# A recurrence followed by a cosine-gated product: the second part in groups of 512 tokens, its down product by halves of the features

## The chip, the cores and the metric

The kernel runs on one core of a Trainium2 chip. The metric is the device time of one execution in microseconds (us). Everything is computed in fp32. The engines are called as in the profile: PE (TensorE, the matmuls; its weight loads are shown apart as PEld), DVE (VectorE), ACT (ScalarE), POOL (GpSimd) and SP (SyncE, which here only issues DMAs).

## What is computed

The first part is a recurrence over 768 steps, for 4 batches and 8 heads of 40 features; its output `y`, turned to 3072 tokens of 320 features, goes through a second part with 2048 hidden features:

```
for t in range(S):                                  # r, k, v, w, a, b: [4, 8, 768, 40]
    y[:, :, t] = einsum('bhd,bhde->bhe', r_t, state)
    Sa = einsum('bhde,bhe->bhd', state, a_t)
    state = state * w_t - einsum('bhd,bhe->bhde', Sa, b_t) + einsum('bhd,bhe->bhde', v_t, k_t)
x = y.transpose(0, 2, 1, 3).reshape(3072, 320)
h = x @ w_in                                        # w_in [320, 2048], w_out [2048, 320]
out = (h * cos(h)) @ w_out
```

## The kernel before, in words

The recurrence goes in 24 chunks of 32 steps. A chunk's 128 partitions are (batch, step), so a chunk is 128 tokens. Three functions do a chunk:

- `prep(c)` does what doesn't need the state: it turns the six operands on PE (tiles `turned`), makes the decays (`wp`, `rw`, `wx` on DVE and POOL), the gram matrices (`gram`, masked into `pc`, `abd`, `rvbd`), and the inverse of a triangular matrix by five levels of squaring. A level is 8 matmuls `power` on PE, a copy on ACT (line 267), mostly an addition on DVE (271) and four 32x32 block transposes on DVE (253), and the next level's matmuls need these transposes.
- `chain(c)` does what needs the state: `x0ps`, `snps`, the state's update `upd`, `sTps`, `mps`, the outputs `yps`, the new state's transpose `strn`, and the seam `xps` (line 382), which turns the chunk's 128 tokens to `xT`, with features in the partitions. The last `xps` of a chunk is used below as the mark of that chunk.
- `mlp(c, xT)` (lines 391 to 424) does the second part for the chunk's 128 tokens. The up product `ph` (399) takes a block of 128 hidden features at a time: three matmuls accumulate over the 320 input features, which are cut in 128, 128 and 64. Each has a 128-column weight tile of `w_in` and a moving operand of 128 tokens. Four blocks fill one PSUM bank of 512 columns, and on these 512 columns the cosine is made: DVE 406, POOL 407, DVE 409 and 410, ACT 411 and 412, DVE 414, which writes `gT`. The down product `po` (416) takes 16 matmuls, each with a 128x128 tile of `gT` as weights and 320 columns of `w_out` moving, all into one bank; ACT copies that to `ot` (421), and four DMAs on SP's queue write it out.

Each fp32 matmul of the program is two passes in the trace (a weight load and a matmul each), so that a `power` level is 16 passes and a chunk's `ph` 96.

The weights arrive as fp64 words. `rounded` (lines 141 to 164) turns each of 28 pieces to fp32: a DMA on ACT's queue into `words`, three operations on DVE, three on POOL, one more on DVE, and a product on POOL into `w_in_sb` or `w_out_sb`.

The loop over c calls `chain(c)`, the loads of chunk c + 2, `prep(c + 1)` and `mlp(c)`. A scheduler then places the instructions in each engine's queue, so that matmuls of `mlp(c)` stand between those of `prep(c + 1)` and of `chain(c + 1)`. Each engine works its queue in order. PSUM has three banks for `prep`, two for `chain`, two for `ph` and one for `po`.

Of the kernel before, what the change touches and what calls it, by code (L numbers as in the profile page):

```python
# [23 lines left out]
def kernel(  # L24
# [39 lines left out]
    # K tiles of the first product of the second part  # L64
# [13 lines left out]
    def kept(name, shape, n=1, fill=None):  # L78
        """Buffers that are used in turn, with a fill that the parts never written keep."""
        tiles = []  # L80
        for i in range(n):
            t = const.tile(shape, F32, tag=f"{name}{i}", name=f"{name}{i}")
            if fill is not None:
                nc.vector.memset(t, fill)
            tiles.append(t)
        return tiles
# [34 lines left out]
    # the strict upper triangle, and of that the blocks on the diagonal  # L121
# [18 lines left out]

    def rounded(dst, src):
# [8 lines left out]
        frac = sb2.tile([P, 512], F32, tag="gT", name="frac")[:n, :cols]  # L150
# [44 lines left out]
    def prep(c):  # L195
        """What of a chunk doesn't need the state."""
# [3 lines left out]
        # products of w over the steps of each batch, by a scan that begins anew at each block  # L200
# [10 lines left out]
        # operands with the decay in them, with steps in the free dimension and in the partitions  # L211
# [13 lines left out]
        # N's transpose, compact, beside what becomes the inverse's transpose: I - N^T  # L225
# [163 lines left out]
    FG = 4  # L389
# [76 lines left out]
```

## Time and profile before

| | |
|---|---|
| time, median of 3 runs | 2125.78 us (2123.2 to 2127.21) |
| span of the profiled execution, first to last instruction | 2120.7 us |
| PE busy | 2016.7 us, 95% |
| PE weight loads | 1713.6 us, 81% |
| DVE, ACT, POOL busy | 936.2, 338.0, 217.5 us |
| mean granted PE clock | 0.70 of full |
| DMA | 40.33 MB, 19 GB/s |

The profile gives no other time of its own execution than the span; the span is 5.1 us under the median of the runs.

How to read it: a row of groups has the line, engine, operation, tiles and shapes, then busy time and mean of one, then the engine's idle time before these instructions and who ended it. The mean of a pass includes its way through the array, which overlaps the next pass; the pace of a stream is its length in a row of the timeline divided by the count, or busy time divided by the count. A row of the timeline has start, length, engine, line, operation, tiles, shapes and count, and in brackets idle time before it. A row of windows has a stretch, then for each engine busy time and number of instructions, then the PE clock granted, as a share of full speed, and DMA.

### The profile page before, as it was taken

To read this page: it belongs to the slowest core of one execution; us is meant where nothing else is said; L and a number is where in the kernel's file an instruction comes from. 1 tells how busy PE (TensorE), PEld (TensorE's weight loads), DVE (VectorE), ACT (ScalarE), POOL (GpSimd) and SP (SyncE) were. 2 spreads that over 40 slices of the span, in tenths; PEclk is the share of its full clock that TensorE was granted. 3 is DMA by queue.
4 is the path that set the end of the run, shared out by engine and by line. 5 is a ranking of instruction groups with operands and counts; after the bars stand their busy time and mean duration, and the time that the engine had idled before them with its cause. 6 is when DMAs were issued, how large, how long until landed. Compare 5 with 4: busy or idle time off the path is not lost.

```text
span 2120.7 us, 35848 instructions
## 1 busy us (share of the span) xinstructions
PE 2016.7 (95%) x15592; PEld 1713.6 (81%) x15592; DVE 936.2 (44%) x1671; ACT 338.0 (16%) x744; POOL 217.5 (10%) x365
## 2 busy tenths in 40 slices
PE   4777999999999999999999999999999999999997
PEld 4766888888888888888888888888888888888885
DVE  8765344343443443444434434444344443444432
ACT  0102112021111111211211102112111021121111
POOL 4662000000000000000000000000000000000000
PEclk8658577586675775866857767677586676776777
DMA  3331010010100100101001000010010000100000
GB/s 83 84 95 26 10 20 12 14 21 4 20 13 14 20 10 14 18 9 20 13 13 20 10 14 13 13 20 13 14 20 9 15 13 13 20 7 1 4 3 4
DMA packets 165211, 40.33 MB, mean 19 GB/s; under 512 B 158656, under 2 KB 161728, under 8 KB 165056
## 3 DMA queue, kind: packets, MB, share of 16 engines
q1 hardware_dynamic: 161280, 27.57, 7.9%
q10 hardware_dynamic: 3776, 10.49, 1.6%
q8 instruction: 123, 2.02, 0.4%
q14 instruction: 32, 0.26, 0.0%
HBM read 34.08 MB, written 3.93 MB: 18 GB/s over the span
## 4 chain that ended last, share of the span: by engine, by line
PE 85%; DVE 10%; ACT 3%; POOL 1%; issue 1%; POOLq 0%; ACTq 0%
PE ph L399 26%; PE power L89 18%; PE po L416 10%; PE yps L89 8%; PE x0ps L89 6%; PE gram L89 5%; PE strn L89 4%; DVE rw L207 4%; PE turned L192 3%; PE snps L89 2%; ACT snbd L308 2%; PE mps L89 1%; DVE wp L205 1%; PE sTps L89 1%; PE xps L382 1%; DVE mbd L346 1%
## 5 line engine op out<-in xcount | busy, mean ns | idle before, releaser
L399 PE MATMUL ph<-xT,w_in_sb 128*128 128x128 f32 (+1 forms) x2304 | 581.7, 388 | 0.5 <-ACT xT L384 0.5
L399 PEld LDWEIGHTS ph<-xT,w_in_sb 128*128 128x128 f32 (+1 forms) x2304 | 436.4, 249 | 134.5 <-issue 83.6
L89 PE MATMUL power<-pc,pbd 128*128 128x64 f32 (+1 forms) x1920 | 392.7, 387 | 25.7 <-DVE pbd L253 25.6
L89 PEld LDWEIGHTS power<-pc,pbd 128*128 128x128 f32 x1920 | 383.1, 305 | 34.3 <-issue 27.0
L416 PE MATMUL po<-w_out_sb,gT 128*128 128x320 f32 x768 | 261.2, 489 | 22.0 <-DVE gT L414 22.0
L253 DVE STREAM_TRANSPOSE pbd<-pc 32x256 f32<-32x256 f32 x480 | 208.4, 434 | 155.3 <-ACT pc L267 146.3
L416 PEld LDWEIGHTS po<-w_out_sb,gT 128*128 128x128 f32 x768 | 158.9, 218 | 91.8 <-DVE gT L414 28.1
L407 POOL TENSOR_SCALAR turns<-turns 128x512 f32<-128x512 f32 x96 | 59.3, 618 | 1193.1 <-DVE turns L406 1193.0
L406 DVE TENSOR_SCALAR turns<-ph 128x512 f32<-128x512 f32 x96 | 66.4, 691 | 210.4 <-PE ph L399 210.4
L267 ACT COPY pc<-power 128x256 f32<-128x256 f32 x96 | 35.8, 372 | 735.2 <-PE power L89 723.8
L271 DVE TENSOR_TENSOR pc<-power,pc 128x256 f32<-128x256 f32 x72 | 30.5, 424 | 275.8 <-ACT pc L267 275.7
L89 PE MATMUL yps<-kn,rvbd 128*128 128x40 f32 x384 | 97.8, 347 | 4.9 <-DVE mbd L346 4.8
L411 ACT ACTIVATE red<-red 128x512 f32<-128x512 f32 x96 | 60.7, 633 | 261.0 <-DVE red L410 261.0
L89 PE MATMUL yps<-bn,mbd 128*128 128x40 f32 x384 | 98.7, 350 | 0.0
L89 PE MATMUL strn<-ident,st 64*64 64x40 f32 x1472 | 96.7, 305 | 0.0
L89 PEld LDWEIGHTS strn<-ident,st 64*64 64x64 f32 x1472 | 93.3, 215 | 2.0
L89 PE MATMUL x0ps<-nat_v,abd 128*128 128x40 f32 x384 | 92.3, 416 | 0.0
L409 DVE SCALAR_TENSOR_TENSOR red<-turns,ph 128x512 f32<-128x512 f32 x96 | 65.8, 685 | 58.2 <-POOL turns L407 58.2
L89 PEld LDWEIGHTS x0ps<-nat_v,abd 128*128 128x128 f32 x384 | 85.3, 327 | 7.5 <-issue 5.4
L89 PEld LDWEIGHTS yps<-kn,rvbd 128*128 128x128 f32 x384 | 78.9, 254 | 11.2 <-DVE mbd L346 9.1
L89 PEld LDWEIGHTS yps<-bn,mbd 128*128 128x128 f32 x384 | 82.0, 264 | 0.0
L207 DVE RECIPROCAL rw<-wp 128x512 f32<-128x512 f32 x24 | 80.4, 3351 | 0.7
(113 smaller groups left out, 2013.8 us busy)
## 6 DMA issues: line engine op xcount, KB each, us to landing
words<-in_moe_w_out_dram ACTq DMA_DIRECT2D x16, 320.0 KB, 3.0
words<-in_moe_w_in_dram ACTq DMA_DIRECT2D x8, 512.0 KB, 4.2
nat_w<-in_w_dram SPq DMA_DIRECT2D x96, 40.0 KB, 2.1
nat_k<-in_k_dram SPq DMA_DIRECT2D x96, 40.0 KB, 2.1
nat_a<-in_a_dram SPq DMA_DIRECT2D x96, 40.0 KB, 2.1
nat_b<-in_b_dram SPq DMA_DIRECT2D x96, 40.0 KB, 2.2
nat_v<-in_v_dram SPq DMA_DIRECT2D x96, 40.0 KB, 2.0
nat_r<-in_r_dram SPq DMA_DIRECT2D x96, 40.0 KB, 2.1
```

Of the source, the lines that this page charges most:

```text
L89: nc.tensor.matmul(o, lhsT=lhsT, rhs=rhs, start=start, stop=stop, skip_group_check=True)
L192: nc.tensor.transpose(ps[:, q, :], x[:, q, :], ident)
L207: nc.vector.reciprocal(seq(rw), wp)
L253: nc.vector.transpose(pbd[blk[i], :, :, blk[i]].rearrange("p e q t -> p (e q) t"), heads(pc)[blk[i], :, 0, :],)
L267: nc.scalar.copy(heads(new)[:, :, 0, :], ps[:, :, 0, :])
L308: nc.scalar.copy(snbd[blk[i], i], ps[blk[i]])
L399: nc.tensor.matmul(ph[:, f, :], lhsT=w_in_sb[: d1 - d0, i, cols], rhs=xT[: d1 - d0, i, :], start=i == 0, stop=i == len(KT) - 1,)
L406: nc.vector.tensor_scalar(n, h, 1.0 / (2.0 * math.pi), ROUND, ALU.mult, ALU.add)
L407: nc.gpsimd.tensor_scalar(n, n, -ROUND, 1.0, ALU.add, ALU.mult)
L409: nc.vector.scalar_tensor_tensor(red, n, -TWO_PI_HI, h, ALU.mult, ALU.add)
L411: nc.scalar.activation(red, red, ACTF.Abs)
L416: nc.tensor.matmul(po, lhsT=gT[:, f, :], rhs=w_out_sb[:, f0 + f, :], start=f0 + f == 0, stop=f0 + f == NF - 1,)
```

## The change

The second part waits until four chunks (512 tokens, one group) are through the seam, and then works for all of them:

- `xT` holds four chunks, `[128, 3, 4, 128]`; `chain` writes its quarter.
- `mlp_up` does one block of 128 hidden features for 512 tokens: three matmuls with a moving operand of 512 columns, in place of twelve with 128. The cosine on 512 columns is as before. A block's `gT` has a buffer of its own, eight in all (`gT0` to `gT7`), each single.
- `mlp_down` does eight blocks for one chunk. The first half of the features is copied from PSUM to `ot` by ACT; the second is added to `ot` by DVE, and the DMAs follow.
- `mlp_part(s)` spreads a group's work over four chunks: up for blocks 0 to 7, down for these (four chunks), up for 8 to 15, down for these. Group 0's parts are called behind chunks 4 to 7, and the last group's parts behind the last chunk.
- To make room, `words` shares the two buffers of `rvbd`, `frac` uses `gT0` and `gT1`, `snT` shares `vT`'s buffer, and the state's update is made in place, without `tmp`.

```diff
-        words = sb2.tile([P, 512, 2], I32, tag="words", name="words")[:n, :cols]
+        words = sb2.tile([P, 512, 2], I32, tag="rvbd", name="words")[:n, :cols]
...
-    def mlp(c, xT):
+    def mlp_up(j, f, xT):
+        ph = ps_h.tile([P, GC * P], F32, tag="h", name="ph")
+        for i, (d0, d1) in enumerate(KT):
+            nc.tensor.matmul(
+                ph, lhsT=w_in_sb[: d1 - d0, i, f * P : (f + 1) * P],
+                rhs=xT[: d1 - d0, i, :, :].rearrange("p c t -> p (c t)"),
+                start=i == 0, stop=i == len(KT) - 1,
+            )
...
+        nc.vector.tensor_tensor(gT_b[j], ph, red, ALU.mult)
+    def mlp_down(g, cc, fh):
+        c = g * GC + cc
+        po = ps_o.tile([P, DM], F32, tag="o", name="po")
+        for j, f in enumerate(range(fh * FH, (fh + 1) * FH)):
+            nc.tensor.matmul(
+                po, lhsT=gT_b[j][:, cc * P : (cc + 1) * P], rhs=w_out_sb[:, f, :],
+                start=j == 0, stop=j == FH - 1,
+            )
+        if fh == 0:
+            nc.scalar.copy(ot_b[cc], po)
+            return
+        nc.vector.tensor_tensor(ot_b[cc], po, ot_b[cc], ALU.add)
...
+    def mlp_part(s):
+        g, cc = s // GC - 1, s % GC
+        if not 0 <= g < NG:
+            return
+        fh = cc // 2
+        if cc % 2 == 0:
+            for j, f in enumerate(range(fh * FH, (fh + 1) * FH)):
+                gT_b[j] = sb1.tile([P, GC * P], F32, tag=f"gT{j}", name="gT")
+                mlp_up(j, f, xT_g[g])
+        else:
+            for i in range(GC):
+                if fh == 0:
+                    ot_b[i] = sb1.tile([P, DM], F32, tag=f"ot{i}", name="ot")
+                mlp_down(g, i, fh)
...
-        mlp(c, xT)
+        mlp_part(c)
+    for s in range(NCH, NCH + GC):
+        mlp_part(s)
```

Where PE's instructions stand then is set by the scheduler. The first place is PE's queue in `prep` of a chunk in the middle, behind the gram matrices, where the levels of `power` begin; before:

```order
L89 MATMUL gram<-rT,vT 128x128 x8
L399 MATMUL ph<-xT,w_in_sb 128x128 x6
L89 MATMUL power<-pc,pbd_138 128x32 x8
L399 MATMUL ph<-xT,w_in_sb 128x128 x9
L89 MATMUL power<-pc,pbd_138 128x64 x8
L399 MATMUL ph<-xT,w_in_sb 128x128 x8
L89 MATMUL x0ps<-nat_v_92,abd 128x40 x4
L89 MATMUL x0ps<-st_152,aT 32x40 x13
L89 MATMUL power<-pc,pbd_138 128x64 x8
```

The same place now, in a chunk that has an up part beside it:

```order
L90 MATMUL gram<-rT,vT 128x128 x8
L401 MATMUL ph<-xT,w_in_sb 128x512 x2
L90 MATMUL power<-pc,pbd_138 128x32 x8
L401 MATMUL ph<-xT,w_in_sb 128x512
L90 MATMUL x0ps<-nat_v_94,abd 128x40 x4
L90 MATMUL x0ps<-st_150,aT 32x40 x16
L90 MATMUL x0ps<-nat_v_94,abd 128x40 x2
L90 MATMUL power<-pc,pbd_138 128x64 x8
L90 MATMUL x0ps<-nat_v_94,abd 128x40 x2
L90 MATMUL x0ps<-st_150,aT 32x40 x5
L401 MATMUL ph<-xT,w_in_sb 128x512 x3
L90 MATMUL power<-pc,pbd_138 128x64 x8
```

And now in the next chunk, which has a down part beside it:

```order
L90 MATMUL gram<-rT,vT 128x128 x8
L422 MATMUL po<-w_out_sb,gT 128x320 x3
L90 MATMUL power<-pc,pbd_138 128x32 x8
L422 MATMUL po<-w_out_sb,gT 128x320 x4
L90 MATMUL power<-pc,pbd_138 128x64 x8
L422 MATMUL po<-w_out_sb,gT 128x320 x4
L90 MATMUL x0ps<-nat_v_92,abd 128x40 x2
L90 MATMUL power<-pc,pbd_138 128x64 x8
L422 MATMUL po<-w_out_sb,gT 128x320 x5
L90 MATMUL power<-pc,pbd_138 128x64 x8
```

Between the levels, runs of 6 to 9 narrow `ph` matmuls have become runs of 1 to 3 wide ones in one chunk and runs of 3 to 5 `po` matmuls in the next. Before, every chunk had its first `po` behind its fourth level.

The second place is PE's queue at the end, behind the last chunk's `yps`; before, with everything up to the last instruction:

```order
L382 MATMUL xps<-ident_154,x 64x128
L399 MATMUL ph<-xT,w_in_sb 128x128 x24
L416 MATMUL po<-w_out_sb,gT 128x320 x4
L399 MATMUL ph<-xT,w_in_sb 128x128 x3
L416 MATMUL po<-w_out_sb,gT 128x320 x4
L399 MATMUL ph<-xT,w_in_sb 128x128 x21
L416 MATMUL po<-w_out_sb,gT 128x320 x8
```

The last rows now, of some forty behind the last `xps`:

```order
L401 MATMUL ph<-xT,w_in_sb 128x512 x6
L422 MATMUL po<-w_out_sb,gT 128x320 x2
L401 MATMUL ph<-xT,w_in_sb 128x512 x3
L422 MATMUL po<-w_out_sb,gT 128x320
L401 MATMUL ph<-xT,w_in_sb 128x512 x3
L422 MATMUL po<-w_out_sb,gT 128x320
L401 MATMUL ph<-xT,w_in_sb 128x512 x3
L422 MATMUL po<-w_out_sb,gT 128x320
L401 MATMUL ph<-xT,w_in_sb 128x512 x3
L422 MATMUL po<-w_out_sb,gT 128x320 x27
```

Before, one chunk's second part stood behind the last `xps`: 48 narrow `ph` and 16 `po` matmuls. Now there are the 48 wide `ph` matmuls of the last group, its 64 `po` matmuls, and 29 `po` matmuls of the group before it.

The third place is ACT's queue in chunk 0, where the DMAs of the weights' words (`words`) stand; before, the third to the seventh of 28:

```order
L223 COPY wxn<-turned 128x320
L146 DMA words<-in_moe_w_in_dram 64x1024
L146 DMA words<-in_moe_w_in_dram 128x1024
L302 COPY x_144<-x0ps 128x4x40 x2
L267 COPY pc<-power 128x8x32
L146 DMA words<-in_moe_w_in_dram 128x1024
L267 COPY pc<-power 128x8x32
L146 DMA words<-in_moe_w_in_dram 64x1024
L267 COPY pc<-power 128x8x32
L146 DMA words<-in_moe_w_in_dram 128x1024
```

And now, the first to the fourth:

```order
L226 COPY wxn<-turned 128x320
L149 DMA words<-in_moe_w_in_dram 128x1024
L305 COPY x_144<-x0ps 128x4x40 x2
L270 COPY pc<-power 128x8x32 x2
L149 DMA words<-in_moe_w_in_dram 128x1024
L270 COPY pc<-power 128x8x32 x2
L149 DMA words<-in_moe_w_in_dram 64x1024
L285 COPY ttbd_140<-pc 32x8x32 x2
L205 COPY w_132<-turned 128x16x31
L206 COPY w_134<-turned 128x16
L311 COPY snbd_148<-snps 32x320 x4
L149 DMA words<-in_moe_w_in_dram 128x1024
```

The words come later and further apart; in DVE's queue the masks of `rvbd` of chunk 1, which share the words' two buffers, now stand behind nearly all 28 pieces.

More of the change, by code (lines that the diff above doesn't have):

```diff
@@ L1 @@
+import itertools
 import math
@@ L149, in rounded @@
         expo = sb2.tile([P, 512], I32, tag="red", name="expo")[:n, :cols]
-        frac = sb2.tile([P, 512], F32, tag="gT", name="frac")[:n, :cols]
+        frac = sb1.tile([P, 512], F32, tag=f"gT{next(turn) % 2}", name="frac")[:n, :cols]
         nc.vector.tensor_scalar(mant, hi, 0xFFFFF, None, ALU.bitwise_and)
@@ new lines, in chain @@
+        return new_st, new_s
+    GC = 4
+    NG = NCH // GC
+    FH = NF // 2
+    gT_b, ot_b = {}, {}
+    def mlp_up(j, f, xT):
[6 more added lines that the diff above has]
+            )
+        n = sb2.tile([P, GC * P], F32, tag="turns", name="turns")
+        nc.vector.tensor_scalar(n, ph, 1.0 / (2.0 * math.pi), ROUND, ALU.mult, ALU.add)
+        nc.gpsimd.tensor_scalar(n, n, -ROUND, 1.0, ALU.add, ALU.mult)
+        red = sb2.tile([P, GC * P], F32, tag="red", name="red")
+        nc.vector.scalar_tensor_tensor(red, n, -TWO_PI_HI, ph, ALU.mult, ALU.add)
+        nc.vector.scalar_tensor_tensor(red, n, -TWO_PI_LO, red, ALU.mult, ALU.add)
+        nc.scalar.activation(red, red, ACTF.Abs)
+        nc.scalar.activation(red, red, ACTF.Sin, bias=half_pi, scale=-1.0)
+        nc.vector.tensor_tensor(gT_b[j], ph, red, ALU.mult)
@@ L429 @@
     load_weights()
+    xT_g = {}
     for c in range(NCH):
-        *state, xT = chain(c, g, *state)
+        if c % GC == 0:
+            xT_g[c // GC] = sb2.tile([P, len(KT), GC, P], F32, tag="xT", name="xT")
+        state = chain(c, g, *state, xT_g[c // GC][:, :, c % GC, :])
         if c + 2 < NCH:
```

43 lines of the change are left out of this document (7 added, 36 removed).

## The prediction

> **What bounds the kernel now.** The page comes first: what is busy, and at which clock.
>
> ```profile
> span 2120.7 us, 35848 instructions
> PE 2016.7 (95%) x15592; PEld 1713.6 (81%) x15592; DVE 936.2 (44%) x1671; ACT 338.0 (16%) x744; POOL 217.5 (10%) x365
> PE   4777999999999999999999999999999999999997
> PEclk8658577586675775866857767677586676776777
> ```
>
> PE is the bound from the fifth slice on, and it has no full clock: the PEclk digits go up and down. The page's means don't say what a pass costs, so the next view is one chunk's period in the middle, cut where the clock changes; then the same stretches for `ph` alone and for `po` alone.
>
> ```profile
> 1110.80:1141.50 30.70, 29.52 (x204) 23.09 (x203) 16.37 (x24) 7.21 (x15) 3.62 (x7) 1.00 0.10 17
> 1141.50:1155.20 13.70, 13.70 (x181) 12.91 (x184) 1.53 (x4) 1.95 (x6) 0.00 (x0) 0.50 0.04 7
> 1155.20:1158.60 3.40, 3.40 (x93) 3.20 (x87) 2.43 (x6) 0.34 (x1) 0.40 (x1) 1.00 0.45 67
> 1158.60:1196.10 37.50, 37.50 (x202) 32.33 (x201) 15.22 (x31) 4.46 (x10) 1.23 (x2) 0.50 0.06 10
> ```
>
> ```profile
> 1110.80:1141.50 30.70, 8.63 (x48) 6.77 (x48) 4.77 (x7) 1.00 0.10 17
> 1155.20:1158.60 3.40, 0.49 (x2) 0.30 (x2) 0.00 (x0) 1.00 0.45 67
> 1158.60:1196.10 37.50, 15.29 (x46) 11.21 (x46) 3.36 (x5) 0.50 0.06 10
> ```
>
> ```profile
> 1110.80:1141.50 30.70, 8.21 (x28) 4.70 (x26) 0.43 (x1) 1.00 0.10 17
> 1158.60:1196.10 37.50, 2.42 (x5) 1.73 (x6) 0.00 (x0) 0.50 0.06 10
> ```
>
> The clock is 1.00 or 0.50, nothing between. A chunk has 34.1 us of the one and 51.2 of the other, 85.3 in all. I count work in full-clock us, halving what ran at 0.50: 34.1 + 25.6 = 59.7, a mean clock of 0.70. Of it `ph` is 8.63 + 0.49 + 15.29/2 = 16.8 (96 passes, 0.175 each), `po` 8.21 + 2.42/2 = 9.4, and the recurrence (`prep` and `chain`) the remaining 33.5, idle time included. So there are two prices to watch, work per pass and clock.
>
> **The pass.** Two rows of the groups by form (busy, mean of one), then the timeline, at the clocks of the rows above (0.50 also for the two PEld rows, whose spacing is 320 columns' pace):
>
> ```profile
> L399 PE MATMUL ph<-xT,w_in_sb 128*128 128x128 f32 x1536 | 386.3, 378 | 0.5 <-ACT xT L384 0.5
> L399 PE MATMUL ph<-xT,w_in_sb 64*128 64x128 f32 x768 | 243.9, 408 | 0.0
> ```
>
> ```profile
> 1114.75 2.32 PE L416 MATMUL po<-w_out_sb,gT 128*128 128x320 f32 x8
> 1176.09 5.21 PE L399 MATMUL ph<-xT,w_in_sb 128*128 128x128 f32 x16
> 2091.54 4.63 PE L416 MATMUL po<-w_out_sb,gT 128*128 128x320 f32 x8 [2.88 <-DVE gT L414]
> 2092.23 0.33 PEld L416 LDWEIGHTS po<-w_out_sb,gT 128*128 128x128 f32 x1 [0.20 <-issue]
> 2094.37 0.33 PEld L416 LDWEIGHTS po<-w_out_sb,gT 128*128 128x128 f32 x1 [0.20 <-issue]
> ```
>
> Four `po` passes start in 2.14 us, 0.535 each: 1.67 ns per column at 0.50, 0.83 at full clock, weight load hidden. A 128-column pass would so stream for 0.107 at full clock; it costs 0.175. Of the three pieces of the 320 features one has 64 rows, and its passes are the dear ones (243.9/768 = 0.318 against 0.251 at the mixed clock): around them the load lies open, I take it. That is 0.068 per pass, 0.41 for a block's six. A 512-column pass streams 0.427 at full clock. I keep the 0.41 per block as it is (per load, not per column); 0 would be the low bound, and 512 columns at the old 0.175 per 128 the high one. An up part (8 blocks, 512 tokens) is 8 x (6 x 0.427 + 0.41) = 23.8; before, two chunks' `ph` were 33.5. A down part is 64 passes of 0.267 = 17.1 and about 0.9 for four bank changes with one `po` bank, each an evacuation (below) partly under other matmuls: 18.0, against 18.8. A pair of chunks then has 2 x 33.5 + 23.8 + 18.0 = 108.8 full-clock us, before 119.4.
>
> ```profile
> L421 ACT COPY ot<-po 128x320 f32<-128x320 f32 x24 | 10.2, 426 | 147.1 <-PE po L416 147.1
> ```
>
> This is the 0.43 us of one evacuation. DVE's addition in place of every second copy, and DMAs that come sixteen at once in every fourth chunk, go beside PE: the loads queued behind them on SP are for two chunks on.
>
> **The clock.** Which work opens and closes the gate?
>
> ```profile
> 1143.62 0.65 PE L89 MATMUL yps<-kn,rvbd 128*128 128x40 f32 x2
> 1147.87 4.24 PE L89 MATMUL strn<-ident,st 64*64 64x40 f32 x64
> 1153.17 1.06 PE L192 MATMUL turned<-ident,rw 128*128 128x128 f32 x4
> 1159.84 4.11 PE L399 MATMUL ph<-xT,w_in_sb 128*128 128x128 f32 x12
> 1172.78 3.51 PE L89 MATMUL power<-pc,pbd 128*128 128x64 f32 x16
> 1193.68 3.59 PE L416 MATMUL po<-w_out_sb,gT 128*128 128x320 f32 x8
> ```
>
> Steps of 3.4 us fit the stretches. By columns streamed and rows used, narrow `ph` fills PE by 0.55 (0.214 of 5.21/16 us, a sixth off for the 64-row passes), `power` by 0.49, `yps` by 0.3, `turned` and `po` by 1. The gate opened after the `turned` and after the `po`, closed in `yps`, and stayed at 0.50 for 37.5 us of `ph`, `power` and `x0ps`, though PE was busy for 37.50 of them. So it opens on a window filled somewhere between 0.55 and 0.85 (the last window had 2.4 us of `po`), and closes somewhere between 0.3 and 0.49. Being busy isn't enough. The Trainium skill (TensorE: Matmul & The Clock Gate, "Part 1: The HAM clock gate") says that the clock has two states, that windows of 3413 ns decide, and that sustained activity opens the gate and an idle window closes it. The two states and the window agree with these rows; as a rule of busy time the rest doesn't, by the row of 37.50 us. By it a pair would take its bare 108.8 us.
>
> Wide `ph` fills more: at half clock a block takes 6 x 0.853 + 0.82 = 5.94 us, fill 0.72 on average, 1 in the 3.4 us of its full-row passes. So walk a pair. All chunks lose 13.7 us at half clock in `yps`, `strn` and `turned`, and some 4 in the gram matrices, unless the gate is open for them. The down chunk then meets 6 `po` passes (3.2), `power` (3.5) and 8 `po` (4.3), which must open it: about 29 at half clock. The up chunk meets one, then two `ph` matmuls (5.6), `power` (3.5), one `ph` and `x0ps` (5.6), `power` (3.5), and three `ph` (5.9) that should open it: 42. Together 71 at half clock, doing 35.5 of the work; the other 73.3 at full clock. A pair takes 144.3, a chunk 72.2.
>
> **Start and end.** The first and last weight, an uncovered level of squaring, and the marks of chunks 0, 1, 22 and 23:
>
> ```profile
> 32.04 1.26 POOL L164 TENSOR_TENSOR w_in_sb<-frac,expo 128x512 f32<-128x512 f32 x1
> 53.24 3.65 PE L89 MATMUL power<-pc,pbd 128*128 128x64 f32 x16 [3.35 <-DVE pbd L253]
> 99.07 0.85 PE L382 MATMUL xps<-ident,x 128*128 128x128 f32 x3
> 173.52 0.87 POOL L164 TENSOR_TENSOR w_out_sb<-frac,expo 128x320 f32<-128x320 f32 x1
> 211.78 0.90 PE L382 MATMUL xps<-ident,x 128*128 128x128 f32 x3
> 1998.13 0.90 PE L382 MATMUL xps<-ident,x 128*128 128x128 f32 x3
> 2072.24 0.90 PE L382 MATMUL xps<-ident,x 128*128 128x128 f32 x3 [0.45 <-DVE x L362]
> ```
>
> The 28 pieces take (173.5 - 32)/27 = 5.2 us each. While `rvbd` of chunk 0 lives, until its `yps` near 90, the words have one buffer, and by their places only three or four pieces come through; the other 24 then take, at 4 to 5.2 us each, until 190 to 215. Chunk 1's `yps`, whose `rvbd` mask stands behind the words, waits for that: its mark stays near 212 although its PE queue is free of the second part. Chunks 2 and 3 have no second part beside them: 85.3 - 24.4 - 10.6 = 50 us of PE, plus five uncovered levels of about 3, at a clock that is mostly half: 65 to 70 each, the first less, since its `prep` is done in the wait. Mark of chunk 3 at 345 (before 212 + 2 x 85.3 = 382; bounds 320 and 370). Twenty intervals of 72.2 follow, the last 11 shorter as now (74.1 in place of 85.3).
>
> Behind the last mark stand 93 `po` matmuls and 16 blocks of wide `ph`. Two banks hold them, each until DVE's product:
>
> ```profile
> 2102.93 0.69 DVE L406 TENSOR_SCALAR turns<-ph 128x512 f32<-128x512 f32 x1 [8.70 <-PE ph L399]
> 2109.26 0.68 DVE L414 TENSOR_TENSOR gT<-ph,red 128x512 f32<-128x512 f32 x1
> ```
>
> From the first of these to the last 7.0 us, so a block every (7.0 + 3.0)/2 = 5 us. 29 `po` (15.5), six blocks (30), 24 `po` (12.8, two blocks under them), six blocks (30), the last block's way (4), 27 `po` (14.4), the output (5): 112, against 48.5 now. With 2.5 of 5 us filled the gate just stays open; closed, a block takes 6.5 us and the tail some 25 us more. The Trainium skill (same page, "A second HAM failure mode: psum-queue depth-cycling") says that short pauses between uses of PSUM banks can make the clock swing; no row of before shows such a tail.
>
> **Sum.** 345 + 20 x 72.2 - 11 + 112 = 1890 of span, and 5 as now between span and median (2120.7 and 2125.78): **1895**.
>
> **Rivals.**
> - *The clock share stays 0.70*: the wide passes save work, and the gate opens no earlier. 108.8/0.70 = 155.4 a pair, 345 + 1554 - 11 + 112 + 5 = 2005. For it: the opening mark isn't known better than 0.55 to 0.85. Against it: `po` stands earlier in every down chunk.
> - *The gate opens right behind the gram matrices in both chunks*: 38 at half clock, 89.8 at full, 64 a chunk: 1731. For it: `turned` opens it now in this chunk; against: gram closed it again within one window.
> - *The gate never closes while PE is busy*: 54.4 a chunk, 1539. The 37.50 us speak against it. This is what the rule of the Trainium skill's page above would give.
> - *Slower: the up chunk never opens its gate*, because `power` and `x0ps` split the wide `ph` into runs of 1 to 3 and its windows stay under the mark. Then (33.5 + 23.8) x 2 = 114.6, and 66 for the down chunk; the tail's blocks at half clock too: 345 + 1806 - 11 + 137 + 5 = 2282. It decides if the mark is above about 0.8.
> - *Slower: the wide pass doesn't save*: it costs four narrow ones, 0.70 at full clock. 67 + 33.6 + 18 = 118.6, at clock 0.70 169.4 a pair, with a tail of 120: 2153. Against it: the 320 columns cost 0.267.
>
> **Numbers.** Forecast 0.60, share 0.70 0.20, early opening 0.09, never closing 0.03, up chunk closed 0.05, no saving 0.03. A difference of 0.2% is about what measuring this kernel can tell from none. The last two share their 0.08 as slower 0.07 and the same 0.01 (no saving, but an earlier opening); the others make faster 0.92. The range goes from 1760, which takes in much of the early opening, to 2020, which takes in the unchanged share and a late start.
>
> **What would show it.** Right: `ph` passes at 0.43 to 0.5 us at full clock; windows that open in `po` or wide `ph` between the levels; chunk pace alternating, the down chunk faster; mark of chunk 3 near 345; some 110 us behind the last mark. Wrong: wide passes at 0.7; up chunks at 0.50 to their end; PE idle for more than a few us per chunk, on `ph` banks or `po`; a weight later than 230.

## The result, and the profile after

| | before | after |
|---|---|---|
| time, median | 2124.49 us (2120.07 to 2127.21, 4 runs) | 1784.41 us (1781.97 to 1787.45, 4 runs) |
| ratio | | 0.841, 95% interval 0.8388 to 0.8432 |
| span of the profiled execution | 2120.7 us | 1784.2 us |

The change makes the kernel faster by 340 us. The forecast was 1895: right in direction and inside its range, 110 us too slow. Runs of one kernel mostly agree within 1%; where some took over 1.5% longer than the shortest, as in four of the experiments, their range stands beside the median.

The page of after, its span, the busy times and the granted clock in 40 slices:

```profile
span 1784.2 us, 32460 instructions
PE 1637.1 (92%) x13864; PEld 1248.0 (70%) x13864; DVE 940.5 (53%) x1695; ACT 346.5 (19%) x744; POOL 220.9 (12%) x365
PEclk9955555679797887877988988887887888887998
```

PE is still the bound, but from the ninth slice on the clock digits are mostly 7 to 9, where before they were 5 to 8. The windows view cuts the span at the marks (last `xps`) of chunks 1, 3 and 23, and the row of before behind it is the same 20 intervals, from the mark of chunk 3 to that of chunk 23:

```profile
0.00:207.30 207.30, 129.04 (x1055) 116.75 (x1055) 139.06 (x252) 20.04 (x47) 102.41 (x147) 0.74 0.32 74
207.30:334.40 127.10, 106.43 (x959) 99.22 (x958) 45.48 (x84) 16.73 (x42) 5.74 (x11) 0.57 0.08 13
334.40:1660.90 1326.50, 1296.97 (x11573) 980.82 (x11573) 708.21 (x1286) 285.78 (x617) 102.84 (x191) 0.83 0.10 16
1660.90:1784.20 123.30, 104.68 (x280) 51.23 (x278) 47.78 (x73) 23.95 (x39) 9.91 (x16) 0.94 0.04 11
```

```profile
384.30:2072.20 1687.90, 1664.04 (x13063) 1414.33 (x13062) 708.17 (x1271) 277.72 (x616) 100.95 (x191) 0.70 0.08 13
```

The record of the clock starts at its first change, here 77.9 us in, and a row counts the time before it as 1.00. Four `turned` take 1.06 us there and 0.66 right after the change, so it was half clock, and the 0.74 of the first row and the first two digits of the page are too high. The other rows lie behind the change.

Work in full-clock us is length times clock. The 20 intervals held 1687.9 x 0.704 = 1189 before and hold 1326.5 x 0.829 = 1100 now (the third digit is the sum over the clock's records). At the old clock 1100 would take 1562. So of the 361 us that these intervals lost, 126 are work and 235 are clock. The rest of the balance: the start is 50 us shorter (334.4 against 384.3) and the end 75 us longer (123.3 against 48.5).

The passes of `ph` by form, as before a row for the full pieces and one for the 64-row piece:

```profile
L401 PE MATMUL ph<-xT,w_in_sb 128*128 128x512 f32 x384 | 231.4, 730 | 6.7 <-DVE gT L415 6.7
L401 PE MATMUL ph<-xT,w_in_sb 64*128 64x512 f32 x192 | 116.1, 686 | 0.0
```

From start to start, in full-clock us over the 20 intervals, a wide pass takes 0.482 (480 passes, 231.5), where four narrow ones took 4 x 0.168. PE waits 6.7 us for `ph` banks in the whole run: the buffers are no bound.

Where does the clock come from? Here is one up chunk (mark at 1054.5) and the beginning of the down chunk (mark at 1128.5) behind it, cut where the clock changes:

```profile
1054.10:1057.50 3.40, 3.40 (x19) 3.28 (x18) 0.00 (x0) 1.93 (x5) 0.00 (x0) 0.50 0.00 0
1057.50:1071.10 13.60, 13.04 (x174) 9.55 (x173) 11.15 (x22) 2.64 (x6) 1.22 (x3) 1.00 0.24 37
1071.10:1078.00 6.90, 6.90 (x33) 4.99 (x31) 3.88 (x8) 1.00 (x2) 0.42 (x1) 0.51 0.17 26
1078.00:1084.80 6.80, 5.12 (x49) 3.35 (x48) 4.14 (x9) 1.38 (x3) 0.62 (x1) 1.00 0.01 1
1084.80:1091.60 6.80, 6.80 (x18) 3.96 (x18) 3.37 (x7) 1.62 (x3) 0.00 (x0) 0.50 0.00 0
1091.60:1118.90 27.30, 27.30 (x194) 16.96 (x193) 21.75 (x33) 8.85 (x17) 5.67 (x10) 1.00 0.08 13
1118.90:1132.70 13.80, 13.80 (x165) 12.44 (x163) 2.89 (x7) 4.23 (x9) 0.00 (x0) 0.51 0.07 13
1132.70:1153.10 20.40, 20.18 (x153) 16.46 (x152) 11.76 (x26) 1.12 (x3) 0.40 (x1) 0.92 0.18 34
```

And the timeline of PE at the places that decide:

```profile
1056.87 0.91 PE L195 MATMUL turned<-ident,rw 128*128 128x128 f32 x4
1058.53 1.12 PE L401 MATMUL ph<-xT,w_in_sb 64*128 64x512 f32 x2
1063.49 1.98 PE L401 MATMUL ph<-xT,w_in_sb 128*128 128x512 f32 x4
1070.69 3.25 PE L90 MATMUL power<-pc,pbd 128*128 128x64 f32 x16
1075.09 4.45 PE L401 MATMUL ph<-xT,w_in_sb 128*128 128x512 f32 x6
1087.14 5.18 PE L401 MATMUL ph<-xT,w_in_sb 128*128 128x512 f32 x6
1136.29 3.41 PE L422 MATMUL po<-w_out_sb,gT 128*128 128x320 f32 x6
```

The gate opens on the `turned` before 1057.5. In the kernel before, it closed again in the gram matrices; now a pair of wide `ph` passes stands among them (1058.53) and four right behind them (1063.49), and it stays open until the first `power` and the `x0ps`. It closes for 6.9 us, the six `ph` passes at 1075.09 open it, it closes once more for 6.8, and then it is open for 27.3 us. In the down chunk six `po` at 1136.29 open it. Over the eight pairs from the mark of chunk 6 to that of chunk 22 an up chunk takes 74.5 us, 28.5 of them at half clock, and a down chunk 59.4, 15.5 of them at half clock.

### The profile page after: what moved, and what is told of

The parts are those of the page before. It is cut to its first block, busy times and chain, and to the rows that moved or that the text cites. A ratio compares the mean times of both kernels' runs of the same rounds, so it can differ in the third digit from the quotient of the medians.

```text
span 1784.2 us, 32460 instructions
## 1 busy us (share of the span) xinstructions
PE 1637.1 (92%) x13864; PEld 1248.0 (70%) x13864; DVE 940.5 (53%) x1695; ACT 346.5 (19%) x744; POOL 220.9 (12%) x365
## 4 chain that ended last, share of the span: by engine, by line
PE 79%; DVE 14%; POOL 2%; ACT 2%; issue 2%; DMA 0%; ACTq 0%; POOLq 0%
PE power L90 16%; PE ph L401 16%; PE po L422 11%; PE yps L90 8%; PE turned L195 6%; PE strn L90 5%; DVE pbd L256 4%; PE x0ps L90 4%; PE gram L90 3%; PE snps L90 3%; PE upd L90 3%; PE mps L90 2%; PE sTps L90 1%; DVE abd L251 1%; PE xps L384 1%
## 5 line engine op out<-in xcount | busy, mean ns | idle before, releaser
L90 PEld LDWEIGHTS power<-pc,pbd 128*128 128x128 f32 x1920 | 297.5, 243 | 129.6 <-issue 112.3
L90 PE MATMUL power<-pc,pbd 128*128 128x64 f32 (+1 forms) x1920 | 307.0, 327 | 78.3 <-DVE pbd L256 77.4
L401 PE MATMUL ph<-xT,w_in_sb 128*128 128x512 f32 (+1 forms) x576 | 342.0, 715 | 6.7 <-DVE gT L415 6.7
L401 PEld LDWEIGHTS ph<-xT,w_in_sb 128*128 128x128 f32 (+1 forms) x576 | 109.7, 217 | 147.3 <-issue 130.0
L90 PE MATMUL yps<-kn,rvbd 128*128 128x40 f32 x384 | 86.7, 315 | 1.9 <-DVE mbd L349 1.9
L90 PE MATMUL yps<-bn,mbd 128*128 128x40 f32 x384 | 87.8, 318 | 0.0
L411 DVE SCALAR_TENSOR_TENSOR red<-turns,ph 128x512 f32<-128x512 f32 x96 | 65.8, 686 | 32.3 <-POOL turns L409 31.5
L90 PEld LDWEIGHTS yps<-kn,rvbd 128*128 128x128 f32 x384 | 69.3, 225 | 10.9 <-DVE gT L415 5.3
L415 DVE TENSOR_TENSOR gT<-ph,red 128x512 f32<-128x512 f32 x96 | 65.3, 681 | 20.4 <-ACT red L414 18.4
L90 PEld LDWEIGHTS x0ps<-nat_v,abd 128*128 128x128 f32 x384 | 65.4, 245 | 13.6 <-issue 9.2
L211 POOL COPY wx<-wp 128x496 f32<-128x496 f32 x24 | 14.7, 614 | 479.3 <-DVE wp L208 433.9
```

The costliest lines, as they stand in the source:

```text
L90: nc.tensor.matmul(o, lhsT=lhsT, rhs=rhs, start=start, stop=stop, skip_group_check=True)
L401: nc.tensor.matmul(ph, lhsT=w_in_sb[: d1 - d0, i, f * P : (f + 1) * P], rhs=xT[: d1 - d0, i, :, :].rearrange("p c t -> p (c t)"), start=i ...
L411: nc.vector.scalar_tensor_tensor(red, n, -TWO_PI_HI, ph, ALU.mult, ALU.add)
L415: nc.vector.tensor_tensor(gT_b[j], ph, red, ALU.mult)
```

## The experiments

The theory after the result: the change gains by the clock more than by the work. The gate weighs a window by columns streamed times rows used, and wide `ph` passes fill their windows where narrow ones, which leave their load open around the 64-row piece, don't. The rival: what helps is the grouping itself (the second part spread otherwise, `po` earlier in its chunks), or fewer and longer passes as such. "Steady" below is the stretch between the marks of chunks 3 and 23, its clock the mean over it.

**The groups without the wide pass.**

```diff
-        for i, (d0, d1) in enumerate(KT):
-            nc.tensor.matmul(
-                ph, lhsT=w_in_sb[: d1 - d0, i, f * P : (f + 1) * P],
-                rhs=xT[: d1 - d0, i, :, :].rearrange("p c t -> p (c t)"),
...
+        for q in range(GC):
+            for i, (d0, d1) in enumerate(KT):
+                nc.tensor.matmul(
+                    ph[:, q * P : (q + 1) * P], lhsT=w_in_sb[: d1 - d0, i, f * P : (f + 1) * P],
+                    rhs=xT[: d1 - d0, i, q, :], start=i == 0, stop=i == len(KT) - 1,
+                )
```

> The group, its parts and the order of po stay as in the changed kernel; each wide up matmul becomes four with 128 columns again. Theory (the gain is mostly the clock, because wide passes keep PE's windows filled in the up chunks): the down chunk keeps its 59.5 us, the up chunk has 67 full-clock us of work at the old share of 0.70, 96 us; a pair takes 155 in place of 133, and the whole about 2010 us, clock share 0.70 to 0.75. Rival (the clock rose because grouping puts po between the levels, and the wide pass saves only its work): the share stays near 0.83, a pair takes 120/0.83 = 144, the whole about 1900 us.

Measured: 2139.7 us (2103.93 to 2141.89, 4 runs; before on that chip 2121.18), within 1% of before and slower than both expected. The trace is of a run of 2140.5. The clock's row of its page has the 5s of before again:

```profile
PEclk8555555669678568568768658768758858755678
```

And its steady stretch, as a row of windows, has before's clock:

```profile
341.50:1968.30 1626.80, 1599.55 (x12980) 1357.93 (x12980) 707.95 (x1286) 284.96 (x616) 102.58 (x191) 0.71 0.08 13
```

The down chunks are nearly as in the change (61.4 us), but an up chunk now takes 100.9 us, 69.3 at half clock. A pair comes to 162.3 us where two chunks took 169 before, so the steady stretch is 61 us shorter and the start 43; the end, 169.8 us in place of 48.5, takes more than that back. So groups alone, with `po` collected in every second chunk, give next to nothing in the whole. In the steady stretch the change is 361 us shorter than before, and by this trace some 300 of these hang on how `ph` runs.

**The 320 features cut evenly.**

```diff
-    KT = [(i, min(i + P, DM)) for i in range(0, DM, P)]
+    KT = [(0, 107), (107, 214), (214, 320)]
...
```

> The 320 input features are cut in 107, 107 and 106 rows in place of 128, 128 and 64; all else as changed. Theory (a change between 128 and 64 rows lays the weight load open): a wide pass falls from 0.48 to 0.43 full-clock us, 576 x 0.05 = 29 full-clock us, 35 us at the mean clock: about 1750 us. Rival (the extra 0.05 is waiting for banks or the change of tile, not the rows): a pass stays at 0.48, the whole within 10 us of 1784.

Measured: 1890 us (1853.75 to 1906.85, 4 runs), and the shortest run is still 69 slower than the change; no expectation had this. The trace is of the longest run, 121 us longer than the change's. Of these, 100 are the start: the mark of chunk 3 comes at 434.6 and not at 334.4, as PE waits for the levels' transposes behind the weights' work on DVE:

```profile
PE power L90 <- DVE pbd L256: 146.9, 46, 23.0
```

```profile
PE power L90 <- DVE pbd L256: 77.4, 48, 8.7
```

(the second row is the change's). DVE in turn sits idle for the words of `w_in`, 115.9 us over 12 waits, where it is 1.0 us in the change (second row):

```profile
  DMA words<-in_moe_w_in_dram: 115.9, 12
  DMA words<-in_moe_w_in_dram: 1.0, 1
```

The records of the transfers show why. Every row of a piece is one packet of 4096 bytes, which takes 0.16 us. The 128 packets of a piece in the change overlap and are through in 2.5 to 3.1 us; the 107 of a piece here start one behind the other and take 17.6 to 18.4 us where no second piece is in flight. So the even cut pays in the transfers, and not on PE. The steady stretch is what matters for the theory: passes of 0.461, without the 64-row form, and yet 1350.6 us at 0.80, no better than the change's 1326.5 at 0.83. It comes up again below.

**Up and down parts mixed.** Every chunk does four blocks up and then these four down, not eight up and eight down in turn; a group has 16 evacuations where it had 8.

```diff
+        for f in range(fq * FQ, (fq + 1) * FQ):
...
+            mlp_up(f % FH, f, xT_g[g])
+        for i in range(GC):
...
+            mlp_down(g, i, fq)
```

> Each of a group's four parts does four blocks up and then these four down for the four chunks, so that every chunk has wide ph and po between its levels; sixteen evacuations of po in a group in place of eight. Theory (the gate opens on what stands between the levels, and the up chunks, 74 us with 30 at half clock, lack po there): half-clock time of a pair falls from 45 to about 30, 7 us less per pair, against some 2 us for evacuations: 1730 to 1750 us, and no more alternation of pace. Rival (alternation costs nothing, since a pair's work is the same): 1785 to 1810 us, by the evacuations alone.

Measured: 1849.35 us (1829.13 to 1863.37, 5 runs), ratio to before 0.8643 (0.8599 to 0.8688): slower than the change, and the expectation was wrong. The steady stretch, in a run of 1861.5:

```profile
330.80:1736.50 1405.70, 1378.17 (x11580) 1031.31 (x11580) 730.82 (x1315) 280.59 (x611) 104.45 (x188) 0.78 0.10 15
```

The chunks no longer alternate (60 to 79 us each), and the clock is 0.78, not 0.83. The loss is clock and not evacuations: the stretch holds 1092 full-clock us, the change's 1100. The three shorter runs (1829 to 1849) show it too, with a clock of 0.764 to 0.776 over the whole, where the change's runs have 0.794 to 0.809. So some `po` in all chunks is worse here than much of it in every second one. That a little of it in each chunk leaves more windows under the mark that opens the gate fits this, but isn't measured.

**The weights in rounds.** Four pieces are rounded before chunk 0's chain, then eight behind each of chunks 0 to 2.

```diff
-    load_weights()
+    load_weights(4)
...
+        load_weights(8)
         mlp_part(c)
```

> The 28 pieces of the weights are rounded four ahead of chunk 0's chain and eight behind each of the chunks 0 to 2, in place of all ahead of it. Theory (chunk 1 waits for the rounding, whose words share rvbd's buffers): the mark of chunk 1 falls from 207 to about 170 and that of chunk 3 from 334 to about 290, the whole to about 1740 us. Rival (the start is bound by uncovered levels of squaring at half clock and by DVE's sum of work): the mark of chunk 3 moves by less than 10 us, the whole stays within 10 us of 1784.

Measured: 1763.83 us (1756.47 to 1773.29), ratio 0.8321 (0.8282 to 0.8361). The mark of chunk 3 is at 292.7, 42 us earlier, as expected, but the time falls by 21 only, between the two expectations, as the steady stretch is longer at a lower clock, with the same instructions:

```profile
292.70:1636.80 1344.10, 1313.91 (x11572) 996.62 (x11572) 710.36 (x1292) 285.88 (x617) 107.34 (x199) 0.82 0.10 16
```

The change has 1326.5 there, and 1333.1 in the trace of its second run (below), so 11 to 18 us are given back. The three hold nearly the same work, 1097, 1100 and 1100 full-clock us, so what differs is the clock. That it goes by where the gate's windows fall on the work is likely, but no run here sets it.

**The gate by itself.** This kernel leaves out all of the reference's work and writes zeros. It runs streams of one shape, each behind 8 us without PE work, or (the last five) behind 32 full passes.

```diff
+    for n in (64, 80, 88, 96, 104, 112, 128):
+        block(f"open{n}", P, P, n, 75)
...
+    block("rows64", 64, P, 512, 20)
+    block("cols64", P, 64, 512, 20)
+    block("zeros", P, P, 512, 20, mv=zero)
+    for n in (32, 40, 48, 56, 64):
+        block(f"close{n}", P, P, n, 120, first=16)
```

> No part of the reference's work: streams of equal fp32 passes on PE, each behind some 13 us of idle, 150 passes of 64, 80, 88, 96, 104, 112 or 128 columns with all rows and weight columns; then 512 columns with all, with 64 rows, with 64 weight columns, and with a moving operand of zeros; then 32 wide passes followed by 240 passes of 32, 40, 48, 56 or 64 columns. At half clock a pass can't take less than its weight load, 0.213 us, so that a stream of n columns fills n/128. Theory (the gate goes by how full the window is): 64 and 80 columns stay at 0.50 to their end, 104 and more open; the mark lies between 0.55 and 0.80; 64 rows of 512 columns (0.5 or less) don't open; the streams that follow the wide passes close at 32 and 40 columns (0.25, 0.31) and stay open at 56 and 64 (0.44, 0.5). Rival (sustained busy time decides): every stream is open after its second window, 64 columns too, and none closes.

The timeline, one row a stream (start, length, tile, rows x weight columns, rows x moving columns, passes):

```profile
99.67 32.30 PE L42 MATMUL ps<-data,w_open 128*128 128x88 f32 x150 [8.14 <-DVE w_open L52]
140.12 20.17 PE L42 MATMUL ps<-data,w_open 128*128 128x96 f32 x150 [8.14 <-DVE w_open L52]
279.23 34.50 PE L42 MATMUL ps<-data,w_rows 64*128 64x512 f32 x40 [8.14 <-DVE w_rows L52]
321.88 20.27 PE L42 MATMUL ps<-data,w_cols 128*64 128x512 f32 x40 [8.15 <-DVE w_cols L52]
350.29 19.77 PE L42 MATMUL ps<-zero,w_zeros 128*128 128x512 f32 x40 [8.15 <-DVE w_zeros L52]
519.09 62.26 PE L42 MATMUL ps<-data,w_close 128*128 128x512 f32 x272 [8.14 <-DVE w_close L52]
589.48 42.95 PE L42 MATMUL ps<-data,w_close 128*128 128x512 f32 x272 [8.14 <-DVE w_close L52]
```

A pass of up to 128 columns takes 0.213 us at half clock and 0.112 at full. 150 passes with 88 columns take 32.3 us, so they stay at half clock, as do 64 and 80; 96 and more open the gate, 5 to 7 us after their start by the clock's record. The record begins with the first of these, at 146.8, so for 64, 80 and 88 it is the pace that shows the half clock. A pass at half clock has room for 128 columns, so the opening mark lies between 88/128 = 0.69 and 96/128 = 0.75. Behind full passes, streams of 32, 40 and 48 columns (the row at 519.09) close the gate after 5 to 6 us, and 56 and 64 (589.48) don't. At full clock a column takes 0.427/512 = 0.00083 us, and 48 and 56 of them fill 0.36 and 0.42 of a pass of 0.112 us: the closing mark lies between these. Passes of 64 rows with 512 columns stay at half clock for all 34 us, though PE never pauses; 64 weight columns, or a moving operand of zeros, open it like the rest. So the gate counts moving columns times rows, not busy time, not values, not weight columns; the rows have one stream here, and the runs below test them further. The Trainium skill's rule of the prediction (TensorE: Matmul & The Clock Gate, "Part 1: The HAM clock gate") has activity against idle windows; the streams at 279.23 and 519.09 are never idle, and yet the one isn't granted the full clock and the other loses it, so here the measurement decides against it.

The marks hold in the kernel too. Columns times rows were summed over the pass records of every window of 3.41 us of before and after. Of 571 windows at half clock, a mark of 0.74 puts all but 14 on the right side, opened above and shut below; with columns alone, without the rows, the best mark misplaces 122. Of 540 at full clock a mark of 0.42 misplaces 48, and without the rows the best one 87.

Wide `ph`, whose third piece has 64 rows, fills 0.83 x 0.427/0.482 = 0.74 on average: just on the mark. That asks for the next test.

**128 rows in every pass.** The third piece gets 64 rows of zeros in `w_in_sb` and in `xT`, which gives the same sums. In the kernel before, nothing else is changed:

```diff
+    nc.vector.memset(w_in_sb[DM % P :, len(KT) - 1, :], 0.0)
+    xT_b = kept("xT", [P, len(KT), P], 2, 0.0)
...
-                        ph[:, f, :], lhsT=w_in_sb[: d1 - d0, i, cols], rhs=xT[: d1 - d0, i, :],
+                        ph[:, f, :], lhsT=w_in_sb[:, i, cols], rhs=xT[:, i, :],
```

> The kernel before with one thing changed: the 64-row third piece of the 320 features is given 128 rows, 64 of them zero in w_in_sb and in xT (two kept buffers), so every ph pass has 128 rows and 128 columns, and the result is the same. Theory (a change of row form lays the weight load open, and the gate counts columns times rows): a narrow pass costs about 0.11 us at full clock in place of 0.164 to 0.175, a chunk 33.5 + 96 x 0.11 + 9.4 = 53.5 full-clock us in place of 59.7; runs of ph then fill their windows by nearly 1 and open the gate between the levels, share about 0.80, 67 us a chunk; mark of chunk 1 stays at 212, then 22 intervals: about 1730 (1690 to 1790), below the change itself, without groups. Rival (narrow passes are dear as such, their loads don't hide): pass stays at 0.16 to 0.175, share at 0.70, time within 30 us of before, 2090 to 2150. Between them (passes get cheap but the gate stays as it is): 53.5/0.70 = 76 us a chunk, about 1930.

In the change likewise, and then with the weights in rounds as well:

> The change with its third piece given 128 rows in the same way, 64 of them zero. Theory: a wide pass costs 0.43 in place of 0.48 full-clock us, 48 of them a pair 2.3 less, so 1.2 a chunk or 28 us over 20 intervals at a share of 0.84; the wide ph then fills its windows by 1, not 0.72, so that the up chunk opens its gate earlier, by 3 to 6 us a pair, another 15 to 30 us: 1735 (1710 to 1760). Rival (the wide ph opened the gate well enough and the exposed loads are no part of it): 1780 to 1795.

> The change with the 128-row third piece and, besides, the weights rounded in rounds (4 pieces before chunk 0's chain, 8 behind each of chunks 0 to 2). Theory: both gains add, as they lie in different stages: mark of chunk 3 near 293, steady chunks as in the kernel with 128 rows: 1700 (1670 to 1735). Rival (the start only shifts the clock's windows, and the gain is given back): no less than the kernel with 128 rows alone.

> The change itself, unaltered, beside the three others on their chip: 1784 within 10 us by every theory.

| one chip | median, us | ratio to before |
|---|---|---|
| before | 2124.51 (7 runs) | |
| before, 128 rows | 1798.29 | 0.8471 (0.8455 to 0.8488) |
| the change again | 1786.06 | 0.8414 (0.8392 to 0.8437) |
| the change, 128 rows | 1696.88 | 0.7983 (0.7956 to 0.8010) |
| the same, weights in rounds | 1659.83 | 0.7827 (0.7794 to 0.7859) |

Before with 128 rows has a single form of `ph` among its groups:

```profile
L401 PE MATMUL ph<-xT,w_in_sb 128*128 128x128 f32 x2304 | 349.9, 313 | 0.5 <-ACT xT L386 0.5
```

Its steady stretch:

```profile
346.20:1758.00 1411.80, 1363.12 (x13063) 1221.23 (x13062) 703.83 (x1271) 277.55 (x616) 100.77 (x191) 0.79 0.10 16
```

Half of the matmul's rows are zeros in a third of the passes, and the kernel before runs within 1% of the change, without groups and without wide passes. The narrow pass falls from 0.168 to 0.117 full-clock us, so the load that lay open was an affair of the 64-row passes; the clock goes from 0.70 to 0.79, as expected. The time missed the expected 1730 by 68, and its range: a chunk holds 56 and not 53.5 full-clock us. Of these 2.5 some 0.7 are the pass (0.117, not 0.11) and 1.2 idle time, since shorter `ph` no longer covers the levels: PE's idle time in the steady stretch is 1411.8 - 1363.1 = 49 us, before 24, and `power` has 25 of it, before none.

The change with 128 rows, its steady stretch and, in an up chunk, the stretch that stays at full clock:

```profile
337.00:1574.40 1237.40, 1204.79 (x11574) 936.37 (x11574) 707.86 (x1286) 285.64 (x617) 102.81 (x191) 0.89 0.11 18
1019.00:1073.60 54.60, 52.20 (x445) 36.75 (x444) 43.79 (x75) 16.58 (x32) 7.93 (x14) 1.00 0.11 17
```

The gate now opens before the gram matrices and holds for 54.6 us; an up chunk takes 66.0 us, 12.3 of them at half clock (28.5 in the change), a down chunk 59.5 as in the change. The gain is 89 us, nearly twice what was expected and beyond the range; by the work it would be 4 full-clock us of 1100, where the expectation had 23. So nearly all is clock. With the weights in rounds the start's gain comes on top, 33 of 37 us: 1659.83, below its expected range too, is the fastest kernel of the study.

**Width, rows and changes of form apart.** Three last kernels on one chip (before there: 2120.17): narrow passes with 128 rows in the change's groups; 96 rows, 32 of them zeros, in the third piece of the wide pass; and before with its pieces in reverse order in every second block.

```diff
...
+                ph, lhsT=w_in_sb[: min(P, d1 - d0 + 32), i, f * P : (f + 1) * P],
+                rhs=xT[: min(P, d1 - d0 + 32), i, :, :].rearrange("p c t -> p (c t)"),
```

```diff
-                for i, (d0, d1) in enumerate(KT):
+                for m, (i, (d0, d1)) in enumerate(list(enumerate(KT))[:: -1 if f % 2 else 1]):
...
```

> The change's groups, but each wide ph matmul is four of 128 columns (as in the narrow run), and the third piece has 128 rows, 64 of them zero (as in the run of the change with 128 rows, which took 1697). It asks what the 512 columns are worth once no row form changes. Theory (what costs is the change of row form, and what opens the gate is columns times rows): four narrow passes cost 4 x 0.117 = 0.47 in place of 0.465, the fill is 0.9 in place of 1, so 1700 to 1730. Rival (long passes hold the gate open by themselves, four times the weight loads in the narrow ones don't): up chunks near 75 us as in the change, about 1790 or more.

> The change with the third piece's passes given 96 rows, 32 of them zero, so that their form still differs from the 128 rows of the others. It parts the two things that 128 rows bring, the hidden load and the fuller window. If the pass stays at 0.48 full-clock us and the fill alone rises from 0.72 to 0.79, above the mark of the stream test: nearly all of the 89 us of the 128-row run come, as 84 of these were clock: 1700 to 1725. If the exposed load is what matters: 1775 to 1790. If the chip takes 96 rows as 128, the pass falls to 0.465 and the time to 1697.

> The kernel before with every second block's three pieces taken in reverse order, so that the 64-row passes of two blocks stand side by side: half as many changes of row form, and the rows as they were. Theory (exposed load at each change, gate with a mark): ph pass from 0.168 to 0.142 full-clock us, 2.5 less a chunk; the fill rises from 0.55 to about 0.63, still under the mark, so the share stays near 0.70 to 0.72: 2020 to 2060. Rival (gains go in proportion to the changes of form that go): half of the way from 2125 to 1798, 1960. Other rival (the 64-row passes cost as such): 2125.

Measured: 1760.1 (ratio 0.8308, 0.8267 to 0.8348), 1708.5 (0.8074, 0.8027 to 0.8121) and 1997.67 (0.9397, 0.9320 to 0.9475; four runs from 1981.9 to 2060.61, the trace is of 2010.7). The steady stretches, narrow first, then 96 rows, then the other order:

```profile
337.70:1627.20 1289.50, 1242.16 (x12980) 1112.12 (x12980) 704.34 (x1286) 283.31 (x616) 102.46 (x191) 0.86 0.11 17
```

```profile
338.20:1586.30 1248.10, 1216.08 (x11574) 947.26 (x11574) 707.81 (x1286) 285.51 (x617) 102.78 (x191) 0.88 0.11 17
```

```profile
377.50:1964.00 1586.50, 1552.47 (x13064) 1344.77 (x13063) 708.20 (x1271) 277.77 (x616) 101.32 (x191) 0.73 0.09 14
```

- *Narrow with 128 rows* lies between the two expectations. Without the 64-row form the groups gain 344 to 382 us on their first version (2103.93 to 2141.89) with the same narrow matmuls; the 512 columns add 63 more. Four passes cost 4 x 0.123 = 0.49, and the fill is 0.107/0.123 = 0.87. Of the 63, 52 lie in the steady stretch, which holds 1109 full-clock us in place of 1096, so that some 14 are work and the rest clock, and 8 lie at the end.
- *96 rows* cost 0.468 a pass, like 128 (0.465) and like the 107 of the even cut (0.461). From start to start at full clock, a wide 128-row pass before a 64-row one takes 0.522 us in the change, and before a 96-row one 0.429: within `ph`, a load lies open only around the 64-row passes. So here are three kernels with the same matmuls, columns and price, and 320, 352 and 384 rows in three pieces: steady 1350.6, 1248.1 and 1237.4 us, at 0.80, 0.88 and 0.89. As the passes cost the same, what parts the first from the other two is the rows; the even cut's fill, 0.83 x 0.427/0.461 = 0.77, is hardly above the change's 0.74, and its clock not above the change's either. The even cut's trace is of its longest run; were all of the 53 us to its shortest in the steady stretch, that would still be 1297. The expectation of 1700 to 1725 for "fill alone" was met, though the pass wasn't the 0.48 that it assumed.
- *The other order* brings the pass to 0.147 (expected 0.142) and was faster than expected by 22 to 62 us in the median: the clock is 0.73, and the chunks take 86, 70 and 80 us in turn, with 58.8, 18.5 and 42.1 of them at half clock. Between shut and open the fill is enough for some chunks and not for others.

## Why the prediction came out as it did

- **What bounds the kernel, and the gate as columns times rows: right.** The forecast's opening mark, 0.55 to 0.85, is 0.69 to 0.75 in the stream test, its closing mark, 0.3 to 0.49, is 0.36 to 0.42. That 64-row passes leave their load open was taken, not known; the runs with 96, 107 and 128 rows show it.
- **The pass: right, its reason in part.** 0.495 was forecast (2.97 a block), 0.482 measured. The open load was taken "per load, not per column", and it is: a 128-row pass before a 64-row one takes 0.205 in place of 0.112 us when narrow and 0.522 in place of 0.429 when wide, 0.093 more in both. But of the 0.41 a block that the forecast kept for the 64-row piece, 128 rows take away only 6 x 0.017 = 0.10. Another 0.23 stays, as in that run a wide pass before a matmul other than `ph` still takes 0.52, the same 0.093 more. So the price came out near by a sum that had its parts wrong, and the expectation of 0.43 for 128 rows fell short. The down part's pass was put at 0.267 and 0.9 for bank changes, 0.281 each; it is 0.318 with its waits (0.284 where another `po` follows, 0.75 before a wide `power`). A pair came to 1326.5 x 0.829/10 = 110.0 full-clock us over the 20 intervals, 108.8 forecast.
- **The clock: the mis-sized term.** The step was "together 71 at half clock" in a pair: 42 in the up chunk, 29 in the down chunk. The eight pairs show 28.5 and 15.5, 44.0 together. A us of half clock costs half a us, so that is 13.5 a pair; with some 3 more of work in these pairs the pair takes 134.0 and not 144.3, ten pairs 103 us. Half of the 27 us lies in each chunk of the pair, and at the same place: the walk kept the gate shut too long behind the gram matrices. In the up chunk it let the gate close "some 4 in the gram matrices" and stay shut until the third level, where "three `ph`" should open it. But `turned` opens it ahead of the gram matrices, and with a pair of wide passes among these the windows from 1057.5 on fill 0.54, 0.43 and 0.41 by the records, so it stays open until the window at 1067.7, with 0.40; a run of six `ph` passes opens it again. In the down chunk the walk had six `po`, `power` and eight `po` at half clock before it opened, some 15 us with the gram matrices. In the trace `turned` opens it there too, it is shut for one window, 3.4 us, and the first six `po` open it. These sums over mixed matmuls are good to some hundredths only and don't tell by themselves which window closes: the one at 1132.6, which does, comes to 0.43, and in the kernel before the one at 1155.2 to 0.46.
- **The rivals.** The slower one with an up chunk that never opens has its condition at a mark above 0.8: it isn't. The run without the wide pass comes nearest to it (100.9 us an up chunk, 69.3 at half clock), though the gate does open there for a third of the time. "Opens right behind the gram matrices in both chunks" (64 a chunk, 1731) was nearer than the forecast, which gave it a chance of 0.09: 67.0 a chunk. With 128 rows it is nearly true (62.8).
- **Start and end.** The mark of chunk 3 came at 334.4 (345 forecast), the last weight at 196.1 (190 to 215). The end takes 123.3 (112 forecast) at a clock of 0.94: the gate does stay open there, and PE is idle for 18.6 us of it. The sum: 1890 - 10.6 - 106.5 + 11.3 = 1784.2.
- **What it took for the cause.** The prediction had the saving per pass and the group's width as one thing. In the runs they part: on one chip, 128 rows without width gain 326 us, width without 128 rows (with the groups) 338, both 428. The two largely do the same: they take the 64-row passes' open loads away or make them few, and lift the fill of `ph` to the mark or over it.

## What to carry to other kernels

Before regrouping work to widen a matmul, look whether its row groups differ: a piece of 64 rows between pieces of 128 cost this kernel as much as its narrow tiles (to mend either alone gave some 330 us), and zeros in the missing rows gave 326 of the 428 for four lines of code. Where the granted clock is the bound, work out the fill of each window (3.4 us here) as columns times rows, and compare it with the marks of a stream test rather than with busy time. A forecast that walks through the windows should carry each open stretch on until a window really falls under the closing mark; work that only holds a gate open counts like work that opens it.

## What the runs showed of the hardware that was not expected

- The gate has two marks, 0.69 to 0.75 to open and 0.36 to 0.42 to close, by moving columns times rows; rows of zeros count, weight columns and values don't. Adding zeros to a matmul made the change 89 us faster at nearly the same price per pass (0.465 and 0.482).
- A wide pass costs the same with 96, 107 or 128 rows (0.468, 0.461, 0.465 full-clock us); the change with its 64-row third piece has 0.482, and narrow passes 0.168 against 0.117. Where 128 rows give way to 64, a pass takes 0.093 us longer, narrow or wide.
- The words of a piece of 128 rows come in 2.5 to 3.1 us, its packets side by side; those of 107 rows take up to 18.4 us, one packet behind the other.
- The same instructions behind another start ran 11 to 18 us longer over 20 intervals (0.82 against 0.83), and two profiles of the change itself differ by 7 us there: the work is the same to 0.3%, the granted clock is not. The place of the gate's windows on the work is the likely reason; no run here tests it.
